# Sliding-window attention and a soft mixture of experts on one core: four-head steps, a single pass of dispatch scores, and a table of sequences

## The chip, the cores and the metric

One NeuronCore of a Trainium2 chip runs the whole program in one launch. The metric is the time of one execution on the device in microseconds. Lower is better. Inputs and outputs are fp32, and lie in the chip's memory (HBM) before and after.

## What is computed

Attention over 4 batches, 8 heads, 768 tokens, 64 values per head, with 4 sink tokens and a window of 128, and then a soft mixture of 8 experts with 4 slots each:

```python
scores = q @ k.T / 8, kept where the key is a sink (0..3) or 0 <= query - key < 128
x = softmax(scores) @ v                      # 3072 tokens x 512
logits = x @ phi                             # 3072 x 32 slots
d = softmax(logits, axis=0)                  # dispatch: over the tokens
c = softmax(logits, axis=1)                  # combine: over the slots
slot_in = d.T @ x                            # 32 x 512
slot_out = relu(slot_in @ w1[e]) @ w2[e]     # 8 experts, F = 1024
out = c @ slot_out                           # 3072 x 512
```

The weights w1 and w2 are 33.5 MB, the queries, keys and values 18.9 MB, the output 6.3 MB.

## The kernel before, in words

The attention is cut into 12 jobs of 256 queries (4 batches times 3, `jobs`). For each job the program adds steps to a planner, `Plan`, in `window_path`:

- `load`: two loads of 128 rows each for keys, for queries and for values, all 8 heads wide (256 KB each). For the first job keys and queries are loaded before the plan, by four heads.
- `prep`: 64x64 transposes of the keys on TensorE into two PSUM banks (32 of them), two copies of 512 columns out of them to `kt`; the same for the queries to `qt`. For later thirds of a batch, a copy of the last 128 key columns to the front, `kt0`. In the first job these are 128x128 transposes.
- `softmax`, four times per job (two halves of the tokens for each four heads, `quad`): scores on TensorE (`S`), mask and row maximum on DVE (`M`), four exponentials on ACT (`E`), then for a pair of them the inverse sums on DVE and the normalisation on POOL or ACT (`N`), and the sinks on POOL (`K0`).
- `weights_transposed` (`T`), `select` (affine selects on POOL that mask the transposed weights) and `sinks_transposed` (`K`).
- `values`: the product with V, one step of 52 fp32 matmuls for all eight heads. Two row groups of the array add into the same banks, so it is done in two passes with a drain of TensorE between them (`go`).
- `natural`: transposes of x back; `Moe.tokens`: the job's dispatch scores and products. `logits` writes the same 32 slots twice into PSUM, once for the plain logits (rows 0 to 63) and once for the exponential (rows 64 to 127); each sums four 128-value pieces of d, so 16 fp32 matmuls. DVE takes the maximum and then the minimum with the running one, ACT copies one half, exponentiates the other with the maximum as bias (`lt`), TensorE transposes `lt`, and `products` gathers d.T @ x, which DVE adds to `acc`.

`Plan.order` sets the order on every engine: it simulates the engines with the costs written at each step, and picks among the ready steps by due times from the table `CFG` (as `'val': [10.65, -12.08, -64.87]`). It keeps PSUM banks in reserve so that no step blocks. `issue` emits the steps in that order, so every engine has a fixed sequence in the program. Steps marked 900 and over are idle matmuls.

After the last job `finish` merges the slots' sums, nine `stack`/`turn` steps split the combine weights on POOL and transpose them on TensorE, and `tail` runs the experts: `first` (w1), `second` (w2) and `combine`, with 32 weight tiles of 1 MB that SP loads in a fixed order between the other loads. Tiles that take over the place of attention's buffers have to wait for the last readers of these (the last `values` for the transposed weights and V). Output leaves in 16 DMAs of 256 KB and 4 of 512 KB.

In the profile all steps of the plan carry line 136, the recorder's line; tiles tell them apart: `first,phi` are the logits, `wt,qt` the scores, `pts` the probabilities, `wt` the transposed weights, keys, V and expert weights, `pst,vsink` the sinks' part of the product with V, `ident,first` the transposes of keys, queries and x, `first,lb` the products.

Of the kernel before, what the change touches and what calls it, by code (L numbers as in the profile page):

```python
# [19 lines left out]
P = 128  # L20
# [47 lines left out]
def gate(nc, plan, c, phi, tmp, name):  # L68

    t = tmp.rearrange("p (k s) -> p k s", k=4)  # L70

    def sort(e):
        for k in range(4):
            nc.vector.tensor_copy(c.phi[:, k, :].rearrange("p (j r s) -> p j r s", j=4, r=2),
                                  t[:, k, :].rearrange("p (r j s) -> p j r s", r=2, j=4))

    plan.add(-1.0, "D", 0.4, lambda e: nc.sync.dma_start(t, phi.rearrange("(c p) s -> p c s", p=P)), w=[name])
    plan.add(7.0, "V", 0.34, sort, r=[name], w=["phi"])


def sink_values(nc, plan, pool, tmp, c, v, v4s):
# [28 lines left out]
    plan.add(1.5, "D", 2.0, load, w=["v4"])  # L110
    plan.add(1.0, "V", 0.9, selectors, w=["srow", "bm"])
    plan.add(1.0, "P", 0.45, lambda e: nc.tensor.matmul(
        h["tile"][:, 0:B * 64], lhsT=tmp[0:32, 512:640],
        rhs=v4.rearrange("p b d -> p (b d)"), start=True, stop=True), r=["srow", "v4"], w=["v4p"], new=h)
    plan.add(1.0, "A", 0.3, lambda e: nc.scalar.copy(hi, h["tile"][:, 0:B * 64]), r=["v4p"], w=["v4h"])
    plan.add(1.0, "V", 0.8, split, r=["v4p", "v4h", "bm"], w=["v4s"], last=h)
# [33 lines left out]
class Plan:  # L150

    LAT, DMA_LAT, SWITCH, STAY = 0.25, 1.8, 0.1, 2.0

    IDLE = 900.0  # L160
    BLOCK, FETCH = 256, 3.9

    def __init__(self, banks):

        self.banks, self.steps, self.modes, self.sizes, self.handles = banks, [], [], [], 0
# [9 lines left out]
    def add(self, key, eng, time, fn, r=(), w=(), new=None, last=None, mode=(128, 128), size=0):  # L175

        self.sizes.append(size)
        self.steps.append((key, eng, time if isinstance(time, tuple) else (time,) * len(eng), fn,
                           tuple(r), tuple(w), self.some(new), self.some(last)))
        self.modes.append(mode if isinstance(mode[0], tuple) else (mode, mode))  # L180

    def order(self):
        steps = self.steps
        writer, readers = {}, {}
        before, opener, later = [], {}, {}
        for i, (_, eng, _, _, r, w, new, last) in enumerate(steps):
            d = set()
            for x in r:
                d.add(writer.get(x, i))
                if x in opener:  # L190

                    d.update(readers.get(x, ())[-1:])
                readers.setdefault(x, []).append(i)
# [6 lines left out]
            for h in new:  # L200
                opener[h["name"]] = i

            for x in r + w:
                if x in opener and eng != "P":
                    o = opener[x]
                    later.setdefault(o, set()).update(y for y in d if steps[y][1] == "P" and y != o)
# [4 lines left out]
        ends = dict.fromkeys(closers, 0.0)  # L211
        nxt, left, ready = [[] for _ in steps], [len(d) for d in before], [0.0] * len(steps)
        for i, d in enumerate(before):
            for x in d:
                nxt[x].append(i)
        free = {"P": 5.3, "A": 5.5, "V": 5.5, "G": 6.8, "D": 3.1}
        todo = {e: [] for e in free}
        banks = dict.fromkeys(range(8), 0.0)
        for i, n in enumerate(left):
            if n == 0:  # L220
                for e in steps[i][1]:
                    todo[e].append(i)
        order, done, mode, place, since = [], set(), (128, 128), 0, 0.0
        while len(order) < len(steps):
            best = None
            for e, o in todo.items():
                at, t0 = [], 1e9
                for i in o:
                    t = max(free[e], ready[i])
                    new = steps[i][6]  # L230
                    if new:
                        free2 = sorted(banks.values())
                        if new[0]["kind"] == "s":
                            m, x = 2, min((max(banks[y], banks[y + 1]) for y in range(0, 8, 2)
                                           if y in banks and y + 1 in banks), default=None)
                        else:
                            m = len(new)
                            x = free2[m - 1] if len(free2) >= m else None
                        if x is None or len(free2) - m < 2 and not later.get(i, done) <= done:
                            continue  # L240
                        t = max(t, x)
                    at.append((t, i))
                    t0 = min(t0, t)
                if at and (best is None or t0 < best[0]):
                    if e == "P":
                        _, t, i = min((steps[i][0] + self.STAY * (self.modes[i][0] != mode), t, i)
                                      for t, i in at if t <= t0 + 0.1)
                    else:
                        _, t, i = min((steps[i][0], t, i) for t, i in at if t <= t0 + 0.02)
                    best = (t0, e, t, i)  # L250
            _, e, t0, i = best
            at = t0
            if e == "P":
                t0 += self.SWITCH * (self.modes[i][0] != mode)
                mode = self.modes[i][1]
            _, engs, times, _, _, _, new, last = steps[i]
            done.add(i)
            for x in engs:
                todo[x].remove(i)
            for h in new:  # L260
# [4 lines left out]
                else:  # L265
                    b = max((x for x in banks if banks[x] <= at + 1e-9),
                            key=lambda x: (x ^ 1 not in banks, banks[x], -x))
# [3 lines left out]
            end = t0 + times[engs.index(e)]  # L271
            place += self.sizes[i]
            if place >= self.BLOCK:
                place -= self.BLOCK
                t = end - (end - t0) * place / self.sizes[i]
# [9 lines left out]
            for x in nxt[i]:  # L285
                ready[x] = max(ready[x], end + (0.05 if steps[x][1] == e else self.DMA_LAT if e == "D" else self.LAT))
                left[x] -= 1
                if left[x] == 0:
                    for y in steps[x][1]:
                        todo[y].append(x)  # L290
# [3 lines left out]
    def issue(self):  # L294
        order = sorted(self.order())
        end = max(t for t, _, i, e in order if e == "P" and self.steps[i][0] < self.IDLE)
        for t, _, i, e in order:
            _, _, _, fn, _, _, new, _ = self.steps[i]
            if t > end and self.steps[i][0] >= self.IDLE:
                continue  # L300
# [16 lines left out]
class InOrder(Plan):  # L317

    at = 2
# [16 lines left out]
class Moe:  # L336
# [25 lines left out]
    def tokens(self, plan, keys, b, j, x, xn, blocks):  # L362
# [11 lines left out]
        both = len(blocks) == 2  # L374
# [964 lines left out]
```

## Time and profile before

| | |
|---|---|
| runs | 231.95, 234.34 and 232.90 us, median 232.9 |
| profiled execution | span 231.4 us, from its first to its last instruction; its own time is not listed beside the runs |
| TensorE busy | 196.0 us, 85% of the span |
| ACT, DVE, POOL busy | 151.9, 147.1 and 126.0 us |
| DMA engines, share of the span | 83.7% on the queue of the loads and stores |
| granted clock of TensorE | 0.969 in the mean |

How to read it: a "busy" time is the union of an engine's instructions. PE is the matmuls, PEld the weight loads, which overlap them; the ends of matmuls are modelled, so short gaps do not show under PE and do under PEld. A window row gives busy microseconds (and instructions) of each engine in a stretch, then the granted clock, the share of the DMA engines and GB/s.

### The profile page before, as it was taken

How to read it: one execution, taken by the hardware profiler on the slowest of the kernel's cores; microseconds unless marked ns; L12 is line 12 of the kernel's file. 1: busy time of each engine (PE TensorE's matmuls, PEld its weight loads, DVE VectorE, ACT ScalarE, POOL GpSimd, SP SyncE). 2: the span in 40 equal slices, each digit the busy share in tenths (PEclk: the TensorE clock that was granted, in tenths of full speed). 3: DMA queues.
4: the chain of work that ended last, by engine and by line, in shares of the span. 5: the costliest groups of instructions: out<-in, count | busy, mean ns of one | idle time of the engine just before them, and what ended most of it. 6: DMA issues, size and time to landing. Idle time of an engine off the chain costs nothing.

```text
span 231.4 us, 9764 instructions
## 1 busy us (share of the span) xinstructions
PE 196.0 (85%) x3912; PEld 144.0 (62%) x3912; DVE 147.1 (64%) x383; ACT 151.9 (66%) x605; POOL 126.0 (54%) x266
## 2 busy tenths in 40 slices
PE   7857998999898999899898889989699999999300
PEld 7836685867676777758577667667476235667200
DVE  5177787796868899797967788689526123017500
ACT  2297898889797987799986889989425113016400
POOL 2029698857769683957967395887973330000000
PEclk9997999999999999999999999999999999999955
DMA  5498969897989699896988889695549999986995
GB/s 114 95 218 200 291 159 302 253 266 203 225 249 241 202 289 322 233 211 211 213 338 197 268 183 298 178 428 224 203 157 423 370 426 390 347 259 224 303 350 227
DMA packets 90921, 59.53 MB, mean 257 GB/s; under 512 B 76532, under 2 KB 84724, under 8 KB 89332
## 3 DMA queue, kind: packets, MB, share of 16 engines
q1 hardware_dynamic: 90868, 58.83, 83.7%
q8 instruction: 33, 0.54, 0.9%
q14 instruction: 20, 0.16, 0.2%
HBM read 52.53 MB, written 6.29 MB: 254 GB/s over the span
## 4 chain that ended last, share of the span: by engine, by line
PE 51%; ACT 17%; DVE 12%; issue 7%; POOL 6%; DVEq 0%; ACTq 0%; POOLq 0%
PE ps L136 50%; ACT pts L136 8%; ACT wt L136 3%; DVE ps L136 3%; DVE small L136 2%; POOL pts L136 2%; ACT first L136 2%; DVE wt L136 2%; POOL wt L136 2%; PE ps L1291 2%; ACT lt L136 1%; DVE vsink L136 1%; DVE qt L136 1%; ACT qt L136 1%; DVE first L136 1%
## 5 line engine op out<-in xcount | busy, mean ns | idle before, releaser
L136 ACT ACTIVATE pts<-ps,small 128x132 f32<-128x132 f32 x192 | 68.1, 392 | 6.1 <-DVE small L136 3.4
L136 POOL TENSOR_SCALAR_AFFINE_SELECT wt<-wt 128x512 f32<-128x512 f32 x88 | 52.8, 634 | 3.0 <-ACT wt L136 1.2
L136 POOL TENSOR_TENSOR pts<-pts,small 128x528 f32<-128x528 f32 x36 | 38.2, 1076 | 29.3 <-DVE small L136 20.9
L136 PE MATMUL ps<-wt 64*64 64x192 f32 (+4 forms) x1278 | 52.5, 298 | 1.6 <-issue 0.3
L136 PEld LDWEIGHTS ps<-wt 64*64 64x64 f32 (+2 forms) x1278 | 38.9, 129 | 12.5 <-issue 4.8
L136 PE MATMUL ps<-wt,qt 64*64 64x196 f32 (+2 forms) x780 | 43.0, 325 | 4.0 <-ACT qt L136 1.4
L136 ACT ACTIVATION_READ_ACCUMULATOR pts<-ps,small 128x1 f32 x192 | 43.9, 229 | 0.0
L136 PEld LDWEIGHTS ps<-wt,qt 64*64 64x64 f32 x780 | 29.7, 135 | 11.3 <-ACT pts L136 2.4
L136 DVE TENSOR_REDUCE small<-ps 128x4 f32<-128x528 f32 x48 | 33.9, 707 | 1.6
L136 ACT COPY wt<-ps 128x512 f32<-128x512 f32 x39 | 23.1, 603 | 8.6 <-PE ps L136 8.5
L136 PE MATMUL ps<-ident,first 64*128 64x64 f32 (+1 forms) x560 | 25.1, 229 | 2.9 <-ACT pts L136 1.4
L136 DVE COPY wt<-ps 128x512 f32<-128x512 f32 x33 | 22.3, 682 | 4.8 <-ACT wt L136 2.1
L136 PEld LDWEIGHTS ps<-ident,first 64*128 64x128 f32 (+1 forms) x560 | 21.8, 141 | 5.2 <-issue 2.6
L136 DVE COPY first<-ps 128x512 f32<-128x512 f32 x24 | 16.4, 682 | 12.7 <-PE ps L136 12.4
L136 PE MATMUL ps<-ident,pts 64*128 64x64 f32 (+1 forms) x396 | 20.2, 233 | 3.7 <-DVE wt L136 2.1
L136 DVE COPY_PREDICATED ps<-later,ps 128x256 f32<-128x256 uint8 x48 | 20.3, 423 | 4.3 <-PE ps L136 3.4
L136 ACT COPY first<-ps 128x512 f32<-128x512 f32 x24 | 14.7, 610 | 12.2 <-PE ps L136 7.3
L136 PEld LDWEIGHTS ps<-ident,pts 64*128 64x128 f32 (+1 forms) x396 | 16.3, 142 | 9.7 <-POOL small L136 5.6
L136 ACT ACTIVATE pts<-pts,small 128x132 f32<-128x132 f32 x48 | 15.9, 437 | 0.6 <-DVE small L136 0.6
L136 PE MATMUL ps<-wt,si 128*32 128x512 f32 x120 | 14.1, 594 | 0.2 <-DVE si L136 0.2
L136 POOL TENSOR_TENSOR small<-pts,small 128x32 f32<-128x32 f32 x48 | 12.1, 252 | 3.9
L136 PE MATMUL ps<-first,phi 128*32 128x128 f32 x384 | 13.0, 276 | 0.1
(122 smaller groups left out, 240.1 us busy)
## 6 DMA issues: line engine op xcount, KB each, us to landing
wt<-in_moe_w_dram SPq DMA_DIRECT2D x26, 1024.0 KB, 6.9
wt<-in_v_dram SPq DMA_DIRECT2D x24, 256.0 KB, 4.5
first<-in_k_dram SPq DMA_DIRECT2D x22, 256.0 KB, 3.7
first<-in_q_dram SPq DMA_DIRECT2D x22, 256.0 KB, 4.7
wt<-in_moe_w_dram SPq DMA_DIRECT2D x8, 512.0 KB, 10.2
out_dram<-wt SPq DMA_DIRECT2D x16, 256.0 KB, 4.5
first<-in_moe_w_dram SPq DMA_DIRECT2D x2, 1024.0 KB
out_dram<-wt SPq DMA_DIRECT2D x4, 512.0 KB, 5.3
```

What stands on the lines that cost most here:

```text
L136: return self.tc.keep_in_program_order(f(*args, **kw))
L1291: nc.tensor.matmul(t[:, 0:P], lhsT=c.ident, rhs=c.ident, start=True, stop=True)
```

## The change

- Keys and queries are loaded by four heads (128 KB each, `load_keys`); one `prep` step transposes keys and queries of four heads together, with four copies of 256 columns instead of two of 512 for each. The first job takes the same path.
- `values` becomes two steps, one per four heads. The first needs neither the sinks nor the other four heads. Each has its own drain.
- `logits` runs once: rows 0 to 63 hold the sum over the first two pieces of d, rows 64 to 127 that over the other two. ACT copies one half to `lt`, DVE adds the halves, negates and takes the running minimum in one operation, reads it out and copies it to the other 64 partitions; ACT then exponentiates from `lt`. The combine softmax works on the negated logits.
- The greedy planner and its `CFG` give way to `ORDER`, a sequence of step numbers for each engine. The 24 idle matmuls before the experts are gone. Costs written at the steps matter for the bank numbers and the emission order only.

```diff
 def logits(e):
-    for a in range(4):
+    for a in range(2):
         for g in range(4):
-            nc.tensor.matmul(L["tile"][32 * g:32 * g + 32, 0:P], lhsT=c.phi[:, a, :],
-                             rhs=xt[:, a, x[g % 2 if both else blocks[0]]], start=(a == 0), stop=(a == 3),
-                             skip_group_check=True)
+            d = 2 * (g // 2) + a
+            nc.tensor.matmul(L["tile"][32 * g:32 * g + 32, 0:P], lhsT=c.phi[:, d, :],
+                             rhs=xt[:, d, x[g % 2]], start=(a == 0), stop=(a == 1), skip_group_check=True)
...
+def total(e):
+    nc.vector.tensor_tensor_reduce(lt[0:64], L["tile"][0:64, 0:P], lt[0:64], -1.0, old[0:64] if n else BIG,
+                                   ALU.add, ALU.min, new[0:64])
+    nc.vector.tensor_copy(new[64:128], new[0:64])
-plan.add(key, "V", 0.2, lambda e: nc.vector.tensor_reduce(
-    new, L["tile"][:, 0:P], op=ALU.max, axis=AX.X, negate=True), r=[L["name"]], w=[("m", n % 2)])
...
-plan.add(next(k), "A", 0.16, lambda e: nc.scalar.copy(lt[0:64], L["tile"][0:64, 0:P]), r=[L["name"]], w=["lt0"])
+plan.add(next(k), "A", 0.16, lambda e: nc.scalar.copy(lt[0:64], L["tile"][64:128, 0:P]), r=[L["name"]], w=["lt0"])
+plan.add(key, "V", 0.32, total, r=[L["name"], ("m", (n + 1) % 2)], w=["lt0", ("m", n % 2)], last=L)
...
+def load_keys(nc, t, src, b, j, quad):
+    for i in range(2):
+        s0 = 256 * j + P * i
+        nc.sync.dma_start(t[:, i, 256 * quad:256 * quad + 256].rearrange("p (h d) -> p h d", h=4),
+                          src[b, 4 * quad:4 * quad + 4, s0:s0 + P, :].rearrange("h p d -> p h d"))
...
+h = turned(keys[0], KIND["kt"], lambda rows, m: kqs[m // 4][rows, m % 2, P * (2 * quad + m // 2 % 2):P * (2 * quad + m // 2 % 2) + P],
+           [("kq", kind, quad) for kind in range(2)])
...
-def go(e):
-    for first in (True, False):
-        if not first:
+def go(e, quad):
+    for turn in range(2):
+        first = turn == quad
+        if turn:
             nc.tensor.drain()
-        for f in (sunk, part) if first else (part, sunk):
-            f(first)
+        for f in ((part, sunk) if turn else (sunk, part)) if quad else (part,):
+            f(*(quad, first) if f is part else (first,))
...
+ORDER = {"P": [
+         10, 11, 8, 12, 21, 9, 13, 35, 27, 38, 14, 16, 46, 7, 94, 49, 15, 2, 107, 100, 57, 110, 118, 60, 121,
...
```

What moves, first on TensorE in the third job, at its product with V (`ps<-wt` with widths 192, 64 and 128, each row four fp32 matmuls; `pst,vsink` is the sinks' part, `first_74` the keys and queries of later jobs, `ident,lt` the transposes of the dispatch scores). Before, from the middle of the product on:

```order
L136 MATMUL ps<-wt 64x192 x4
L136 MATMUL ps<-wt 64x64 x4
L136 MATMUL ps<-wt 64x128 x4
L136 MATMUL ps<-pst,vsink 128x256 x2
L136 MATMUL ps<-ident,lt 128x128
L136 MATMUL ps<-ident,first_74 128x64 x32
L136 MATMUL ps<-first_75,lb 32x257 x4
L136 MATMUL ps<-ident,pts 128x64 x16
```

and now, from the end of the first four heads' part to behind the second's:

```order
L136 MATMUL ps<-wt 64x128 x4
L136 MATMUL ps<-ident,first_74 128x64 x16
L136 MATMUL ps<-pst,vsink 128x256 x2
L136 MATMUL ps<-wt 64x192 x4
L136 MATMUL ps<-wt 64x64 x4
L136 MATMUL ps<-wt 64x128 x4
L136 MATMUL ps<-wt 64x192 x4
L136 MATMUL ps<-wt 64x64 x4
L136 MATMUL ps<-wt 64x128 x4
L136 MATMUL ps<-pst,vsink 128x256 x2
L136 MATMUL ps<-ident,first_74 128x64 x16
L136 MATMUL ps<-ident,lt 128x128
```

One block of 32 transposes of keys and queries behind the product has become two of 16, one between its two parts and one behind it.

Second, on TensorE from the merge of the slots' maxima (`sums,si`) to the experts (`wt,si`; `ident,pts` and `ident,qt` are the turns of the combine weights, `lt,acc` the slots' inputs, plain `ident` idle matmuls). Before:

```order
L136 MATMUL ps<-sums,si 128x1
L136 MATMUL ps<-ident,pts 128x128 x2
L136 MATMUL ps<-ident,lt 128x128
L136 MATMUL ps<-ident,qt 128x128 x2
L136 MATMUL ps<-first_75,lb 32x257 x4
L136 MATMUL ps<-ident,pts 128x128 x2
L136 MATMUL ps<-ident 128x128 x3
L136 MATMUL ps<-lt,acc 128x64 x2
L136 MATMUL ps<-rz,phi 128x1
L136 MATMUL ps<-wt,si 32x512 x48
```

and now:

```order
L136 MATMUL ps<-sums,si 128x1
L136 MATMUL ps<-ident,lt 128x128
L136 MATMUL ps<-first_75,lb 32x257 x4
L136 MATMUL ps<-ident,pts 128x128 x2
L136 MATMUL ps<-lt,acc 128x64 x2
L136 MATMUL ps<-ident,pts 128x128 x6
L136 MATMUL ps<-ident,qt 128x128 x4
L136 MATMUL ps<-ident,pts 128x128 x2
L136 MATMUL ps<-ident,qt 128x128 x2
L136 MATMUL ps<-rz,phi 128x1
L136 MATMUL ps<-wt,si 32x512 x48
```

Seven of the nine turns (14 transposes) now stand between the slots' inputs and the experts, where none stood; the idle matmuls are gone.

Third, on SP from the last loads of keys and queries (`first_74<-in_k_dram`, `in_q_dram`) to the outputs; a weight tile is one row `wt<-in_moe_w_dram` or `first...<-in_moe_w_dram`, and two halves of the last form, `128x4x256`. Before:

```order
L136 DMA first_74<-in_k_dram 128x8x64 x2
L136 DMA first_74<-in_q_dram 128x8x64 x2
L136 DMA wt<-in_v_dram 128x8x64 x2
L136 DMA wt<-in_moe_w_dram 128x2x1024
L136 DMA wt<-in_v_dram 128x8x64
L136 DMA first_74<-in_moe_w_dram 128x2x1024
L136 DMA wt<-in_moe_w_dram 128x2x1024
L136 DMA wt<-in_moe_w_dram 128x2048 x2
L136 DMA wt<-in_v_dram 128x8x64
L136 DMA wt<-in_moe_w_dram 128x2048 x4
L136 DMA first_75<-in_moe_w_dram 128x2048
L136 DMA wt<-in_moe_w_dram 128x2048 x5
```

and now:

```order
L136 DMA first_74<-in_q_dram 128x4x64 x2
L136 DMA wt<-in_v_dram 128x8x64
L136 DMA wt<-in_moe_w_dram 128x2x1024 x3
L136 DMA wt<-in_v_dram 128x8x64
L136 DMA wt<-in_moe_w_dram 128x2x1024
L136 DMA wt<-in_v_dram 128x8x64
L136 DMA wt<-in_moe_w_dram 128x2x1024
L136 DMA wt<-in_v_dram 128x8x64
L136 DMA wt<-in_moe_w_dram 128x2x1024 x2
L136 DMA wt<-in_moe_w_dram 128x2048 x4
L136 DMA first_74<-in_moe_w_dram 128x2048
L136 DMA wt<-in_moe_w_dram 128x2048
```

Both end with `first_75`, five tiles and eight halves. Before, 13 tiles are issued ahead of the last keys and queries and 18 ahead of the last V; now it is 9 and 14.

## Rows read from the trace of the kernel before

**Rows 1.** The page: span, and each engine's busy us, share and instructions.
```profile
span 231.4 us, 9764 instructions
PE 196.0 (85%) x3912; PEld 144.0 (62%) x3912; DVE 147.1 (64%) x383; ACT 151.9 (66%) x605; POOL 126.0 (54%) x266
```
**Rows 2.** Windows: us, busy (x) of PE, PEld, DVE, ACT, POOL; clock, DMA share, GB/s.
```profile
8.00:20.00 12.00, 7.74 (x140) 6.05 (x140) 7.89 (x25) 9.54 (x43) 4.15 (x8) 0.97 0.65 148
20.00:160.00 140.00, 128.64 (x2995) 99.41 (x2991) 112.45 (x270) 121.79 (x510) 103.73 (x210) 0.99 0.88 252
160.00:177.80 17.80, 15.35 (x293) 11.53 (x293) 9.80 (x30) 8.29 (x26) 13.04 (x32) 1.00 0.63 227
177.80:231.40 53.60, 37.84 (x454) 20.50 (x454) 13.83 (x33) 10.64 (x26) 3.83 (x7) 0.90 0.90 325
```
**Rows 3.** Waits from 20 to 160 us: PEld, in total, times, longest.
```profile
PEld ps L136 <- issue: 10.8, 36, 1.5
PEld ps L136 <- ACT pts L136: 6.1, 16, 1.0
PEld ps L136 <- POOL small L136: 5.6, 10, 1.0
PEld ps L136 <- POOL wt L136: 3.6, 7, 0.7
```
**Rows 4.** Groups by form: busy us, mean ns of one, idle before.
```profile
L136 PE MATMUL ps<-first,phi 128*32 128x128 f32 x384 | 13.0, 276 | 0.1
L136 ACT COPY wt<-ps 128x512 f32<-128x512 f32 x39 | 23.1, 603 | 8.6 <-PE ps L136 8.5
L136 DVE COPY wt<-ps 128x512 f32<-128x512 f32 x33 | 22.3, 682 | 4.8 <-ACT wt L136 2.1 <-PE ps L136 2.0 <-POOL small L136 0.6
L136 ACT CAST pts<-ps 128x256 fp32r<-128x256 f32 x3 | 1.1, 374 | 1.8 <-PE ps L136 1.8
L136 DVE CAST pts<-ps 128x256 fp32r<-128x256 f32 x3 | 1.2, 413 | 0.0
L136 ACT ACTIVATE pts<-pts,small 128x132 f32<-128x132 f32 x48 | 15.9, 437 | 0.6 <-DVE small L136 0.6
L136 POOL TENSOR_TENSOR pts<-pts,small 128x528 f32<-128x528 f32 x36 | 38.2, 1076 | 29.3 <-DVE small L136 20.9 <-ACT pts L136 6.7 <-ACT call L136 1.8
L136 DVE TENSOR_REDUCE sums<-ps 128x1 f32<-128x128 f32 x12 | 3.4, 285 | 3.0 <-PE ps L136 2.6 <-ACT pts L136 0.5
L136 DVE SCALAR_TENSOR_TENSOR acc<-acc,sums,ps 128x257 f32<-128x257 f32 x11 | 5.2, 472 | 1.0 <-PE ps L136 0.9
L136 ACT COPY lt<-ps 64x128 f32<-64x128 f32 x12 | 3.1, 258 | 1.6 <-DVE sums L136 1.6
```
**Rows 5.** Timeline of the weight loads: start us, us, behind a product's drain.
```profile
79.28 0.85 PEld L136 LDWEIGHTS ps<-wt 64*64 64x64 f32 x29 [0.35 <-issue]
```
**Rows 6.** Timeline of SP: start us, us, loads of keys, queries, phi.
```profile
1.51 0.42 SPq L1280 DMA_DIRECT2D first<-in_k_dram  x1
5.27 0.51 SPq L1280 DMA_DIRECT2D first<-in_q_dram  x1
11.21 0.99 SPq L136 DMA_DIRECT2D first<-in_k_dram  x2
```
**Rows 7.** Timeline of TensorE: first transposes, end of the last job, experts.
```profile
7.81 0.60 PE L136 MATMUL ps<-ident,first 128*128 128x128 f32 x4
175.96 0.44 PE L136 MATMUL ps<-ident,pts 128*128 128x128 f32 x2
208.78 1.93 PE L136 MATMUL ps<-wt 128*32 128x256 f32 x32
```
**Rows 8.** Windows at the experts: the columns of rows 2.
```profile
165.00:170.00 5.00, 3.78 (x104) 2.88 (x106) 1.01 (x3) 0.50 (x3) 4.47 (x11) 1.00 0.03 8
190.00:195.00 5.00, 5.00 (x55) 1.96 (x45) 1.72 (x5) 1.26 (x3) 0.00 (x0) 1.00 1.00 410
206.00:208.70 2.70, 2.70 (x36) 1.97 (x28) 1.20 (x3) 0.95 (x2) 0.00 (x0) 1.00 0.32 104
```

More of the change, by code (lines that the diff above doesn't have):

```diff
@@ L175, in add, with depends @@
     def add(self, key, eng, time, fn, r=(), w=(), new=None, last=None, mode=(128, 128), size=0):
[L177 to L186, printed above, removed]
+        self.steps.append((key, eng, time if isinstance(time, tuple) else (time,) * len(eng), fn, tuple(r), tuple(w),
+                           self.some(new), self.some(last), mode if isinstance(mode[0], tuple) else (mode, mode), size))
+    def depends(self):
+        writer, readers, before = {}, {}, []
+        for i, (_, _, _, _, r, w, new, _, _, _) in enumerate(self.steps):
             d = set()
+            opens = {h["name"] for h in new}
             for x in r:
                 d.add(writer.get(x, i))
-                if x in opener:
+                if x in self.opened:
                     d.update(readers.get(x, ())[-1:])
@@ L199, in order @@
             before.append(d)
[L200 to L206, printed above, removed]
+            self.opened |= opens
+        return before
+    def order(self):
+        steps, self.opened = self.steps, set()
+        before = self.depends()
+        nxt, left, ready = [[] for _ in steps], [len(d) for d in before], [0.0] * len(steps)
+        for i, d in enumerate(before):
+            for x in d:
+                nxt[x].append(i)
         closers = {}
@@ L210, in order @@
                 closers[h["name"]] = closers.get(h["name"], 0) + 1
[L211 to L223, printed above, removed]
+        ends, free, banks = dict.fromkeys(closers, 0.0), dict(self.START), dict.fromkeys(range(8), 0.0)
+        todo = {e: list(reversed(o)) for e, o in ORDER.items()}
+        on = {i: e for e, o in ORDER.items() for i in o}
+        order, mode, place, since = [], (128, 128), 0, 0.0
         while len(order) < len(steps):
@@ L226, in order @@
             for e, o in todo.items():
[L227 to L243, printed above, removed]
@@ L256, in order @@
[L256 to L259, printed above, removed]
+                if not o or left[o[-1]]:
+                    continue
+                i = o[-1]
+                t, new = max(free[e], ready[i]), steps[i][6]
+                if new:
+                    if new[0]["kind"] == "s":
+                        x = min((max(banks[y], banks[y + 1]) for y in range(0, 8, 2) if y in banks and y + 1 in banks), default=None)
+                    else:
+                        x = sorted(banks.values())[len(new) - 1] if len(banks) >= len(new) else None
+                    if x is None:
+                        continue
+                    t = max(t, x)
@@ L260, in order @@
+                if best is None or t < best[0]:
+                    best = (t, e)
+            at, e = best
+            i, t0 = todo[e].pop(), at
+            _, eng, times, _, _, _, new, last, modes, size = steps[i]
+            time = times[eng.index(e)]
+            if e == "P":
+                t0 += self.SWITCH * (modes[0] != mode)
+                mode = modes[1]
             for h in new:
@@ L294, in issue @@
     def issue(self):
[L295 to L300, printed above, removed]
+        for _, _, i, e in sorted(self.order()):
+            _, _, _, fn, _, _, new, _, _, _ = self.steps[i]
             for h in new:
@@ L814, in load @@
         b, j = jobs[n]
[L815 removed]
+        s0 = 256 * j
         if kind == 2:
[L817 to L827 removed]
@@ L829, in prep @@
[L829 to L840 removed]
+            x = (2 * n + i) % 4
@@ L881, in softmax @@
+                add(keys[1 + 2 * kind + x], "AV", (0.27, 0.33), out, r=[h[x]["name"]],
+                    w=[("q" if kind else "kt", quad, x)], last=h[x])
+        if j == 0:
+            add(keys[6], "G", 0.22, lambda e: nc.gpsimd.tensor_copy(
+                ktb[:, a, 1:3, 0:4], ktb[:, a, 1:2, 4:8].to_broadcast([P, 2, 2, 4])),
+                r=[("kt", quad, 0)], w=[("kts", quad)])
     def softmax(keys, n, tl):
@@ L1103, in window_path @@
     for i in range(NSLOT - 7):
-        add(O["w"][0] + O["w"][1] * i, "D", 3.0, lambda e: weight())
-    add(100.0, "D", 3.0, lambda e: weights.load(moe.first[0]), w=[("kq", x, i, y) for x in range(2) for i in range(2) for y in range(2)])
-    add(100.0, "D", 3.0, lambda e: weight(),
-        w=["kt0", ("kts", 0), ("kts", 1), "v4s"] + [("kt", i, y) for i in range(2) for y in range(2)])
-    add(100.0, "D", 0.0, lambda e: moe.place(
+        add((f"w.{i}", 0, 0.0), "D", 2.6, lambda e: weight())
```

328 lines of the change are left out of this document (119 added, 209 removed), and 53 rows, old and new, of the table ORDER.

## The prediction, before the changed kernel ran

> **What bounds the kernel now.** I read the page first, then windows by stage, the waits of the middle stage, the groups by form, and last the timelines of single steps.
>
> The page [rows 1] shows TensorE busy for 85% of the span and no other engine over 66%. The windows [rows 2] show where. From 20 to 160 us, eleven of the twelve jobs, TensorE is busy 128.6 of 140 us (92%), ACT 121.8 (87%), DVE 112.5, POOL 103.7, and the DMA engines 88%. From 8 to 20 us TensorE has 4.3 us idle, in the last job (160 to 177.8) 2.4. So before the experts start at 177.8 it stands still for 11.4 + 4.3 + 2.4 = 18.1 us in all, and whatever shortens its own work in the middle is worth nearly its full length. The reader should also look at the weight loads, since ends of matmuls are modelled: PEld is busy only 99.4 of the 140 us. What ends its idle time [rows 3] is spread: 10.8 us "issue", then waits of a few tenths for probabilities on ACT (6.1), sinks on POOL (5.6), selects on POOL (3.6). There is no one late engine. The experts and the output, 177.8 to 231.4, are TensorE until some 2 us past 208.78 [rows 7] and mostly DMA afterwards; the change edits nothing in there but the order of the tiles.
>
> **The change part by part.** The sum is made against the profiled span of 231.4. The runs have a median of 232.9, so 1.5 is added at the end; the lowest run, 231.95, would make that 0.6.
>
> *Logits.* 384 records in 12 groups of 32 become 192. They are 13.0 us busy [rows 4], 1.08 a job. Half is 6.5 us of TensorE. At the 92% at which the engine is busy I count 5.9 as path: -5.9.
>
> *Product with V in two.* The matmuls stay, but there are two drains per job instead of one. The one drain shows as a gap of 0.35 us in the weight loads [rows 5]; some of it may be covered by matmuls still running, so twelve more cost between 0 and 4.2 us. I take 3.0, nearer to the row: +3.0. So half of what the logits give is handed back. Each drain is paid by TensorE itself; nothing else can run in it.
>
> *First job and start-up.* 16 transpose records of 128 columns (the last four took 0.60 from 7.81 [rows 7]) become 32 short ones, about even. More important, keys and queries of the second job can be loaded as soon as four heads of the first are transposed, about 8.5 us, where SP issued them at 11.2 [rows 6] behind phi and five loads of values. In the 4.3 us of idle time from 8 to 20 I give this 2: -2.0 (bounds 0 and -4.3).
>
> *Copies.* 48 copies of 512 columns become 96 of 256. ACT takes 0.60 for 512 and 0.37 for 256, DVE 0.68 and 0.41 [rows 4]. The order gives ACT 46 instead of 24 (+2.6 us) and DVE 50 instead of 24 (+4.2). ACT also takes five more of the 512-column copies of x (+3.0, DVE -3.4), but 16 fewer normalisations of 15.9/48 = 0.33 each (-5.3); those go to POOL as four of 1.08 (+4.3), and the boundary copies `kt0` are now halves, at most 0.5 each by POOL's rate for 528 columns, which adds up to 4 us more there. ACT comes out even, DVE at +1, POOL at +4 to +8. What hides it is their idle time from 20 to 160, 18, 27 and 36 us [rows 2]. Without that cover DVE and POOL would cost what they add.
>
> *Running maximum.* No row shows the fused operation. It reads PSUM and SBUF at 128 columns; the nearest rows are the reduction of 128 columns, 0.285, and the three-operand operation of 257, 0.472 [rows 4]. I take 0.3, with a read-out and a 64-row copy of at most that each. Twelve jobs then have 6 to 10.8 us of it on DVE where the reductions had 3.4, at most 7.4 more, hidden as above. The chain is longer: ACT's copy (0.26 [rows 4]) ran beside the reduction and now goes first, so the exponential starts about 0.5 later. Queued behind the waiting operation on DVE are the masks of the next scores, for which ACT's exponentials wait; on TensorE scores stand between logits and transposes, which covers it in the middle. In the last job nothing does: +0.5.
>
> *Packing.* What is left is the order. The first four heads' product no longer waits for the last selects or the sinks, keys and queries of four heads are replaced while the other four are in use. That touches the waits on POOL's selects and sinks and part of those on ACT [rows 3], 9.2 to 15.3 us of weight-load idle, of which perhaps half is true idle of TensorE. Bounds: zero, and the whole 11.4 us idle of the middle. I take 4.5, nearer to the rows on POOL: -4.5.
>
> *End.* Seven turns now stand between the slots' inputs and the experts. A turn is two transposes, 0.44 us alone and 0.30 when packed (four took 0.60) [rows 7], so seven are 2.1 us. They left the gaps between the steps of this chain, where TensorE now waits, so they count up to their length; against that stands the copy of the slots' inputs to SBUF, which they cover, and what TensorE waits there now: +0.5 (bounds -0.5 and +2.1). The shorter logits of the last job are counted above.
>
> *Weights.* 9 tiles instead of 13 are issued ahead of the last keys and queries, 14 instead of 18 ahead of the last V. The DMA engines idled at 3% from 165 to 170 [rows 8], so two of the four fit there (1.05 MB at 410 GB/s [rows 8] is 2.6 us), if their buffers are free then, and more before it. The last tiles land shortly after 206 and are used at 208.78 [rows 7, 8]: 2 us of slack. I take +0.5, between 0 and the 8 of the rival below.
>
> Sum: -5.9 + 3.0 - 2.0 + 0.5 - 4.5 + 0.5 + 0.5 = -7.9. The span would be 223.5, the median of the runs 225.0.
>
> *A rule against it.* The eight loads of 128 KB at the start were issued 0.54 apart, from 1.51 to 5.27 [rows 6], and the transposes of the last of them ran at 7.81 [rows 7]: all were in within some 2 us of the last issue, so they overlapped. The change makes 88 loads of this size out of 44 of 256 KB. The Trainium skill (DMA: Bandwidth & Descriptors, "Anatomy of one DMA" and "Rules for kernel authors") asks for 1 MB and more per DMA and gives about 2 us fixed for each on its software-issued path; paid one after the other, 44 more would be 88 us by estimate. By the rows the fixed part overlaps, and the sum has nothing for it.
>
> **The rivals.**
>
> *TensorE stands between the two parts (slower).* Its sequence is fixed: when the first part is done and 16 transposes behind it, the second waits for the selects of the other four heads, whatever else is ready. POOL runs these last and has 4 to 8 us more to do. For it: the waits on POOL's selects exist already, 3.6 us in 7 times, 0.5 each [rows 3]. Against: POOL has 36 us of slack. Price: 0.6 us in each of 11 jobs, +6.6, and the packing gain of 4.5 does not come: 231.4 - 7.9 + 4.5 + 6.6 = 234.6, runs 236. It decides from an average wait of 0.3 at the second part: with the packing gone that leaves 3.3 + 4.5 against 7.9, no gain.
>
> *The weights come late.* Four tiles more behind the last V are 10.2 us of DMA. If their buffers are only freed by the last product with V, they do not fit into the idle time, and the expert products stall by 10.2 - 2 = 8 us; TensorE's gain is then hidden by the transfers: 231.4 - 8.4 + 8 = 231.0, runs 232.5. For it: from 177.8 on the DMA engines are 90% busy [rows 2]. Against: most of these tiles have buffers of their own. One tile late costs at most 0.6.
>
> *The order packs better.* If two thirds of the 18.1 us of idle time go, that is 12 instead of 6.5: 218, runs 219.5. For it: the steps are finer everywhere. Against: twelve jobs with waits of 0.3 to 0.6 on four engines need a nearly perfect agreement of planned and real times.
>
> *The order does nothing.* Logits and drains alone, -2.9, and +1.5 of the small terms, without a gain at the start: 230, runs 231.5. Here the change does its work on TensorE but the idle time moves elsewhere.
>
> **How the numbers follow.** Forecast, 222 to 229 in the runs: 0.55. Better packing: 0.14. No gain from the order: 0.09. Late weights: 0.08. Standing between the parts: 0.14. About 1% is what a measurement of this kernel tells from no change, 2.3 us. Faster by over 1% (below 230.6): the forecast and the better packing with a fifth of the next two cases, 0.73. Within 1%: most of these two, 0.12. Slower: 0.15, nearly all from the rival at TensorE. The range from 218.5 to 234 leaves out the far end of the better packing and most of the slower case.
>
> **What would show it.** Right: TensorE's busy time before the experts falls by some 3 to 5 us, logits show 192 records and 6.5 us; weight loads show two gaps of about 0.35 per product; the experts start near 170; idle time of TensorE before that falls from 18 to about 12. The fused maximum takes 0.3 to 0.5 on DVE. Wrong: a row of waits of TensorE on POOL's selects of some 6 us or more (first rival); stalls of TensorE on "issue" or DMA while `wt,si` or the `128x256` matmuls of the experts run, with the DMA engines full (second); experts at 175 or later with no single wait (last). The forecast fails as well if the jobs' pace is set by ACT, busy over 92% from 20 to 150.

## The result, and the profile after

| | before | after |
|---|---|---|
| median of 20 runs each, us | 234.09 | 231.58 |
| lowest to highest | 231.75 to 238.25 | 228.64 to 236.28 |
| ratio, 95% interval | | 0.9868 (0.9835 to 0.9902) |
| profiled execution: its time, span | span 231.4 | 230.66, span 228.9 |

The change makes the kernel 1.3% faster, where I had forecast 3.4% (225.0). Shares and ratios below are of runs taken beside runs of the kernel before; executions that were disturbed are left out of the ratios.

The page of the changed kernel, as [rows 1]:

```profile
span 228.9 us, 9482 instructions
PE 198.2 (87%) x3730; PEld 138.1 (60%) x3730; DVE 149.0 (65%) x413; ACT 153.4 (67%) x620; POOL 133.1 (58%) x281
```

Its windows in the stretches of [rows 2] (busy us of PE, PEld, DVE, ACT, POOL; clock; DMA share; GB/s):

```profile
8.00:20.00 12.00, 10.70 (x194) 7.58 (x194) 10.23 (x31) 9.68 (x45) 4.73 (x11) 1.00 0.66 149
20.00:160.00 140.00, 131.82 (x2948) 97.52 (x2949) 116.52 (x305) 127.11 (x535) 117.61 (x238) 1.00 0.86 237
160.00:177.80 17.80, 12.71 (x118) 7.10 (x122) 7.39 (x26) 4.65 (x15) 5.68 (x16) 0.72 1.01 415
177.80:228.90 51.10, 36.48 (x445) 19.75 (x434) 12.10 (x26) 10.29 (x25) 3.84 (x7) 0.90 0.89 314
```

TensorE is busier up to 160 us, and from 160 to 177.8 it does little, at a granted clock of 0.72 in the mean where it had 1.00. So I cut both traces at events instead: the end of the last product with V, the experts' first matmul, the experts' last `128x256` group. Before:

```profile
8.00:170.60 162.60, 145.06 (x3332) 111.86 (x3331) 125.69 (x307) 135.35 (x564) 116.70 (x236) 0.99 0.83 236
170.60:177.85 7.25, 6.68 (x89) 5.13 (x90) 4.51 (x16) 4.26 (x13) 4.22 (x12) 1.00 0.98 375
177.85:208.78 30.93, 30.93 (x386) 15.06 (x387) 6.75 (x22) 5.01 (x16) 3.83 (x7) 1.00 0.97 355
208.78:231.40 22.62, 6.91 (x69) 5.44 (x68) 7.03 (x12) 5.62 (x12) 0.00 (x0) 0.76 0.82 283
```

and after:

```profile
8.00:161.15 153.15, 143.66 (x3161) 105.94 (x3161) 126.75 (x335) 136.78 (x578) 122.86 (x249) 1.00 0.85 232
161.15:175.03 13.88, 8.79 (x78) 5.48 (x76) 6.33 (x23) 4.65 (x15) 5.15 (x14) 0.74 1.01 416
175.03:207.37 32.34, 32.34 (x387) 15.08 (x386) 6.11 (x19) 4.66 (x15) 3.84 (x7) 0.96 0.91 333
207.37:228.90 21.53, 6.91 (x69) 5.45 (x68) 7.04 (x12) 5.64 (x12) 0.00 (x0) 0.77 0.85 296
```

The whole result is in these rows. Attention, up to the end of the last product with V, is 9.45 us shorter; the way from there to the experts is 6.63 longer (13.88 against 7.25); the experts are 1.41 longer, the output 1.09 shorter. The sum is -2.5, the difference of the spans. The gain came, and two thirds of it were given back within 14 us.

Where it was given back shows on TensorE's timeline (`lt,acc` are the slots' inputs, `ident,pts` and `ident,qt` the turns of the combine weights, `wt,si` the experts):

```profile
160.77 0.38 PE L136 MATMUL ps<-pst,vsink 64*128 64x256 f32 x2
166.03 0.44 PE L136 MATMUL ps<-ident,pts 128*128 128x128 f32 x2
166.75 0.66 PE L136 MATMUL ps<-lt,acc 128*128 128x64 f32 x4 [0.29 <-DVE acc L136]
167.48 0.54 PE L136 MATMUL ps<-ident,pts 128*128 128x128 f32 x2
169.93 1.12 PE L136 MATMUL ps<-ident,pts 128*128 128x128 f32 x4 [1.91 <-POOL pts L136]
172.43 0.69 PE L136 MATMUL ps<-ident,qt 128*128 128x128 f32 x2 [0.95 <-POOL qt L136]
174.22 0.66 PE L136 MATMUL ps<-ident,qt 128*128 128x128 f32 x2 [0.33 <-ACT pts L136]
175.03 11.91 PE L136 MATMUL ps<-wt,si 128*32 128x512 f32 x96
```

and on POOL's, which splits the combine weights that TensorE then turns:

```profile
160.14 0.46 POOL L136 TENSOR_TENSOR pts<-call,pts 128x128 fp32r<-128x128 f32 x1
166.60 0.29 POOL L136 CAST pts<-call 128x128 fp32r<-128x128 f32 x1 [6.00 <-PE ps L136]
171.54 0.29 POOL L136 CAST qt<-call 128x128 fp32r<-128x128 f32 x1 [1.67 <-PE ps L136]
```

The slots' inputs are done at 167.41 and in SBUF at 167.74, so the experts could have begun less than a microsecond after them, as they do in the first experiment below. They stand behind the last turn in TensorE's sequence. The nine splits share three places in SBUF; a split may only overwrite a place after the turn that reads it. POOL had made two by 160.6 and then stood 6.00 us, because the second turn comes behind the last job's products in TensorE's fixed sequence (166.03). Seven splits were left, and POOL and TensorE took turns waiting for each other.

Windows of this stretch after, for the clock:

```profile
164.00:166.00 2.00, 0.95 (x10) 0.32 (x10) 1.54 (x7) 1.45 (x5) 0.00 (x0) 1.00 1.03 426
166.00:168.00 2.00, 1.64 (x12) 0.92 (x8) 1.47 (x5) 0.00 (x0) 1.24 (x4) 0.92 1.00 414
168.00:170.00 2.00, 0.09 (x2) 0.07 (x2) 1.01 (x3) 0.36 (x1) 1.72 (x5) 0.50 1.02 414
176.00:178.00 2.00, 2.00 (x16) 0.47 (x12) 0.09 (x2) 0.00 (x0) 0.00 (x0) 0.52 0.85 360
```

The granted clock is 0.50 (1.2 of 2.4 GHz) from 168 to 176. It fell shortly before 168, after TensorE had worked 0.95 of 2.00 us from 164 to 166 and 1.64 from 166 to 168; behind the fall stands the emptiest row, 0.09 us. A turn then takes 0.63 to 0.69 instead of 0.44 [rows 7], and the experts' first 96 matmuls 11.91 instead of 10.51.

Groups and waits that answer to [rows 3] to [rows 5]. PEld's waits from 20 to 160 us, the groups by form, and the weight loads behind the two drains of one job:

```profile
PEld ps L136 <- issue: 17.1, 60, 0.8
PEld ps L136 <- ACT pts L136: 4.7, 18, 0.8
PEld ps L136 <- POOL wt L136: 3.1, 7, 0.8
PEld ps L136 <- POOL small L136: 1.6, 5, 0.4
```

```profile
L136 PE MATMUL ps<-first,phi 128*32 128x128 f32 x192 | 7.7, 277 | 0.5 <-DVE first L136 0.3 <-DVE wt L136 0.2
L136 DVE CUSTOM_DVE_ANT_0 lt<-ps,lt,sums 64x128 f32<-64x128 f32 x11 | 3.7, 337 | 2.5 <-ACT lt L136 1.3 <-ACT sums L136 1.2
L136 DVE DVE_READ_ACCUMULATOR2_ANT sums<- 64x1 f32 x12 | 0.9, 75 | 0.0
L136 DVE COPY sums<-sums 64x1 f32<-64x1 f32 x12 | 1.8, 147 | 0.4
```

```profile
86.75 0.65 PEld L136 LDWEIGHTS ps<-wt 64*64 64x64 f32 x24 [0.34 <-issue]
89.38 0.65 PEld L136 LDWEIGHTS ps<-wt 64*64 64x64 f32 x24 [0.35 <-issue]
```

The waits for probabilities, sinks and selects fell, those on "issue" rose by 6.3 us with 24 more of them. The two gaps of 0.34 and 0.35 within one product are its two drains; the rows do not say what else the 24 are. The fused maximum is 0.34, with read-out and copy 0.56.

One more difference lies at the start. The granted clock of the kernel before fell there, behind waits of TensorE of 1.43 us (ahead of 16.48) and 0.97 (ahead of 18.16):

```profile
18.00:20.00 2.00, 1.42 (x28) 1.31 (x30) 1.76 (x9) 2.00 (x9) 1.92 (x4) 0.82 0.86 198
20.00:22.00 2.00, 1.88 (x33) 1.50 (x33) 1.29 (x3) 1.36 (x4) 1.76 (x7) 0.50 1.00 223
22.00:24.00 2.00, 2.00 (x40) 1.42 (x36) 1.23 (x3) 0.35 (x2) 2.00 (x5) 0.82 1.16 263
```

The changed kernel has 1.00 in all three.

### The profile page after: what moved, and what is told of

The parts are those of the page before. It is cut to its first block, busy times and chain, and to the rows that moved or that the text cites. A ratio compares the mean times of both kernels' runs of the same rounds, so it can differ in the third digit from the quotient of the medians.

```text
span 228.9 us, 9482 instructions
## 1 busy us (share of the span) xinstructions
PE 198.2 (87%) x3730; PEld 138.1 (60%) x3730; DVE 149.0 (65%) x413; ACT 153.4 (67%) x620; POOL 133.1 (58%) x281
## 5 line engine op out<-in xcount | busy, mean ns | idle before, releaser
L136 PE MATMUL ps<-wt 64*64 64x192 f32 (+5 forms) x1262 | 59.3, 300 | 4.7 <-DMA wt<-in_v_dram 1.0
L136 PEld LDWEIGHTS ps<-wt 64*64 64x64 f32 (+3 forms) x1262 | 40.3, 129 | 17.9 <-issue 8.3
L136 POOL TENSOR_TENSOR pts<-pts,small 128x528 f32<-128x528 f32 x40 | 42.3, 1071 | 14.3 <-DVE small L136 12.8
L136 ACT COPY wt<-ps 128x512 f32<-128x512 f32 (+1 forms) x49 | 24.1, 509 | 10.2 <-PE ps L136 8.7
L136 DVE COPY wt<-ps 128x256 f32<-128x256 f32 (+1 forms) x47 | 24.9, 536 | 6.5 <-ACT wt L136 3.7
L136 PE MATMUL ps<-ident,first 64*128 64x64 f32 x576 | 26.1, 228 | 1.1 <-DMA first<-in_k_dram 1.0
L136 PEld LDWEIGHTS ps<-ident,first 64*128 64x128 f32 x576 | 21.3, 140 | 7.5 <-issue 2.6
L136 DVE COPY first<-ps 128x512 f32<-128x512 f32 x19 | 12.9, 685 | 9.3 <-PE ps L136 8.4
L136 PE MATMUL ps<-wt,si 128*32 128x512 f32 x128 | 15.6, 642 | 0.0
L136 POOL COPY wt<-wt 128x256 f32<-128x256 f32 (+1 forms) x21 | 6.8, 327 | 11.3 <-ACT wt L136 8.5
L136 ACT ACTIVATE pts<-pts,small 128x132 f32<-128x132 f32 x32 | 10.5, 421 | 0.7 <-DVE small L136 0.7
```

Of the source, the lines that this page charges most:

```text
L136: return self.tc.keep_in_program_order(f(*args, **kw))
```

## Experiments

The theory: attention gained what was forecast, and the turns took it, by POOL's waits and the low clock they cause. Rivals: the weights are the limit at the end; the last job's own chain is; the attention gain is something else than logits and order. The last is tested for the logits and the drains alone: no run separates the four-head steps and loads, the product in two and the new table from one another.

**The turns spread over the last job.** Edit of the changed kernel's table, ends of two sequences (copies follow the same order):

```diff
 "P": [
...
-898, 899, 836, 956, 905, 838, 902, 917, 910, 912, 959, 921, 965, 962, 971, 974, 977, 968, 980, 924
+898, 899, 836, 956, 959, 905, 974, 838, 902, 965, 917, 962, 977, 910, 971, 912, 968, 980, 921, 924
 "G": [
...
-955, 958, 964, 973, 970, 961, 976, 967, 979
+955, 958, 973, 964, 961, 976, 970, 967, 979
```

> The changed kernel with the nine turns of the combine weights spread between the last job's steps (five of them ahead of the slots' inputs, and the other copies and splits in the same order), nothing else. Theory (the turns behind the slots' inputs ate the gain): POOL makes its splits from 159 to about 167 with no wait over 1 us for TensorE, the experts' first matmul starts at 168 to 170 instead of 175.0, the granted clock stays at 1.0 until there, span 222 to 224, time 5 to 7 us below the changed kernel's 231.6. Rival 1 (the weights are the limit: the DMA engines are full from 158 to 176): the experts start early but stand still for weights, time 229 to 231. Rival 2 (the last job's chain is the limit, not the turns): the experts start at 173 or later, time within 1 us of 231.6.

Measured: 227.39 us, ratio 0.9754 (0.9698 to 0.981), span 225.7. TensorE:

```profile
166.87 0.66 PE L136 MATMUL ps<-lt,acc 128*128 128x64 f32 x4
168.35 10.51 PE L136 MATMUL ps<-wt,si 128*32 128x512 f32 x96
192.31 5.08 PE L136 MATMUL ps<-wt 128*32 128x256 f32 x57 [1.97 <-DMA wt<-in_moe_w_dram]
```

POOL's longest wait of the row (0.55 us; another of 0.30):

```profile
161.31 0.29 POOL L136 CAST pts<-call 128x128 fp32r<-128x128 f32 x1 [0.55 <-PE ps L136]
```

The experts start 6.7 us earlier, with a full clock and their 96 matmuls at 10.51. Attention ends 0.6 earlier (160.54); the way from there to the experts is 7.81 instead of 13.88, near the 7.25 of the kernel before. So the turns were the cause, and the first part of the theory holds. But the span falls by only 3.2, less than I expected. The 96 matmuls end 8.1 us earlier (178.86 against 186.94), the last `128x256` group starts 3.1 earlier (204.30 against 207.37): 5.0 us are lost in between. There TensorE stands for weights, 2.2 us in all around 190, and the granted clock falls behind that wait to 0.60 and 0.54 (192 to 196). The first rival was not what limited the changed kernel, but it is the next limit.

**One turn alone.** Of the same edit only step 959 (the turn for which POOL waited 6.00) moved behind 956, its copy with it.

> The changed kernel with one step moved: the turn for whose room POOL waits 6.0 us is put right behind the turn ahead of it, with its copy. If that one wait is the cause, POOL's wait goes and the experts start at 170 or earlier, time 226 to 227. If it is the whole row of turns behind the slots' inputs (each split waits for the turn before it in its room), POOL does two more splits early and then waits for the next turn until about 167.5: the experts start at 173.5 to 175, time within 1.5 us of 231.6.

Measured: 233.06 us, ratio 0.9931 (0.9886 to 0.9975). POOL:

```profile
166.69 0.29 POOL L136 CAST pts<-call 128x128 fp32r<-128x128 f32 x1 [1.39 <-PE ps L136]
173.56 0.29 POOL L136 CAST pts<-call 128x128 fp32r<-128x128 f32 x1 [5.26 <-PE ps L136]
```

The wait splits into 1.39 and 5.26; the experts start 14.6 us after the last product (13.9 without the edit). One wait removed shows the next in the same row. (In this profiled execution attention ends 4.7 us later, at 165.85, with 2.6 us of TensorE's waits for loads of queries between 66 and 84 us, so only its end is compared.)

**Idle matmuls instead.** Eleven matmuls of the identity put into the waits of the changed kernel's last stretch, no turn moved.

> The changed kernel with 11 idle matmuls (128 columns, as the kernel before had) in TensorE's waits of the last stretch: 3 ahead of the last products, 5 behind the third turn, 2 and 1 between later turns. Theory (the granted clock fell to 0.5 there because TensorE had nothing to do, and that made turns 0.63 instead of 0.44 and the experts' first 96 matmuls 11.9 instead of 10.5 us): the clock stays at 1.0 up to the experts, these start 0.5 to 1.5 us earlier and their 96 matmuls take 10.5; time 2 to 3 us below 231.6. If the clock falls anyway, or the idle matmuls delay the turns by what they save: within 1 us.

Measured: 228.75 us, ratio 0.9812 (0.9749 to 0.9875), span 225.9.

```profile
173.63 10.51 PE L136 MATMUL ps<-wt,si 128*32 128x512 f32 x96 [0.47 <-DVE qt L136]
```

```profile
168.00:170.00 2.00, 1.11 (x11) 0.92 (x10) 1.31 (x6) 0.36 (x1) 1.11 (x3) 1.00 1.03 414
```

The clock stays at 1.00 through the stretch, the 96 matmuls take 10.51, and the way from the last product to the experts is 13.1 instead of 13.9. By the trace that is 2.2 us (1.4 + 0.8) of the 3.0 by which the span is shorter; most of the rest is attention. The ratio's interval overlaps that of the changed kernel. The low clock was part of the loss. The removal of the idle matmuls alone does not bring it, the waits do: of the 24 steps the kernel before ran three here (0.83 us at 176.24), and with the turns spread none runs and the clock is 1.00 from 160 to 190.

**Weights earlier.** Three tiles taken from behind the last V and planned at 75, 84 and 96 us (with the turns spread they are issued at 76.3, 87.9 and 97.5), first with the turns spread, then with the changed kernel's own turns:

```diff
 "D": [
...
-937, 542, 484, 406, 543, 541, 544, 617, 485, 618, 558, 615, 616, 696,
+937, 542, 944, 484, 406, 543, 541, 544, 939, 617, 485, 618, 558, 615, 616, 935, 696,
```

> The turns spread as in the first experiment (227.4 us, span 225.7), and three weight tiles of 1 MB that already had buffers of their own taken from behind the last loads of V to the idle stretches of the DMA engines at 75, 84 and 96 us. Theory (with the turns gone from the path, the weights are next: TensorE stood 2.2 us for DMA and the engines were full from 155 to 201): the waits on weights go, the last expert products end 2 to 2.5 us earlier, span about 223.3, time 225. Rival (the early tiles collide with the loads of keys and queries of jobs 8 and 9, and these with TensorE): attention ends 1 to 2 us later, time 227 to 229.

> The changed kernel with the same three tiles moved, and the turns left as they are. If the changed kernel's end was limited by turns and not by weights: no gain, 231.6 within 1 us. If late weights were the cause of the lost gain (my rival of late weights): 3 us or more faster.

Measured with the turns spread: 225.40 us, ratio 0.9663 (0.9604 to 0.9722), span 222.0; no wait of TensorE on weights is left. Attention ended 1.4 us later than without the tiles (161.91), as the rival had it, but the time was the theory's.

```profile
190.00:200.00 10.00, 10.00 (x180) 6.16 (x171) 0.65 (x2) 0.77 (x2) 0.00 (x0) 1.00 1.01 323
```

Without: four runs from 229.96 to 237.47, too scattered for a ratio; the profiled span is 228.0 against 228.9, the experts start 13.9 us after the last product as before, and take 12.15 for the 96. So the same three tiles are worth 2.0 us by the medians once the turns are off the path (3.7 by the two profiled spans, but 223.79, the time of the one with tiles, is the lowest of its six runs; the intervals of the two ratios overlap); with the turns still on it they are worth no more than a microsecond by the profiled spans. A variant with two tiles at 84 us instead:

> As the turns with early weights (225.4 us, span 222.0), but the tile that stood at 75 us moved to 84, so that two tiles lie in the longest idle stretch of the DMA engines (84 to 90 us). There the fifth product with V ended 2 us later than without it (79.1 against 77.1) and attention 1.4 later in all. If that early tile held up the loads of queries: attention ends at about 160.5 instead of 161.9, span 220.5 to 221.5, time 224. If two tiles in a row hold up the next loads of V and queries instead: the same or 1 us slower.

Measured: 226.21 us, 0.9668 (0.962 to 0.9716): no difference. Attention ended at 163.3, not earlier; the second alternative.

**The scores twice, and a third drain.** Two edits of the changed kernel that take one term of the sum back each: `for a in (0, 1, 0, 1)` in `logits`, and a `drain` ahead of the second part of the product.

> The changed kernel with each job's dispatch scores issued twice into the same bank (16 fp32 matmuls as before the change, the second eight overwrite the first). If TensorE sets the pace in the middle (my term of -5.9 for the logits): +6 us, time 237.5, between 236.5 and 238.5. Rival (another engine sets the pace, ACT is busy 91% of the middle): 0 to +2.

> The changed kernel with one more drain of TensorE per job, between the two parts of the product with V. My term: 0.25 each, +3.0 us in all (bounds 0 and +4.2). If the drains are covered by matmuls that still run, or by waits at the second part that come anyway, 0 to +1.

Measured: 236.21 us, ratio 1.0112 (1.0031 to 1.0193), which is 0.0244 or 5.7 us over the changed kernel; by the profiled span +4.0 (232.9). The third drain: 234.13 us, 0.9972 (0.9918 to 1.0026), 0.0104 or 2.4 us over it. In the trace of the doubled scores attention ends 2.9 us later (164.04). Together the intervals leave about 2 us on either side of the 5.7 and 1.5 of the 2.4 (an estimate from the ratios above). So the scores are worth 4 to 6 us in the new order and a drain per job some 2.4, near the 5.9 and 3.0 of the sum.

**The scores once, in the old order.** The kernel before with its planner and only `tokens` and the sign of the combine softmax exchanged:

> The kernel before with its planner, its step times and its eight-head steps, and of the change only the dispatch scores issued once with the fused running maximum. If the logits' term (-5.9) holds by itself: 234.1 - 5.5 = 228.5, between 227.5 and 230. If the old order turns the saved TensorE time into other waits: 231 to 234.

Measured: 246.83 us, ratio 1.0544 (1.0485 to 1.0602). A planner may have made a new order of it, so the next kernel has the old sequences written out, and only the operations in them changed:

> The kernel before with every engine's sequence frozen as its planner made it (the same steps in the same places on every engine, banks by the same simulation), and of the change only the dispatch scores issued once, with the fused running maximum in the place of the two reductions. TensorE is 6.5 us less busy. If my logits term holds by itself, without a new order: the end of the eleventh product with V moves from 160.3 to about 155.5, time 234.1 - 5.5 = 228.5. If the fixed order keeps TensorE waiting at the same places for the other engines, and only a new order turns shorter steps into time: 232 to 234, with more waits of TensorE on ACT and POOL. The previous run without a frozen order (246.8) was the planner's new order then, not the operations.

Measured: 248.92 us, ratio 1.0607 (1.0545 to 1.0668). So a loss of this size needs no new order: the operations in the old sequence are enough. ACT and DVE of this kernel around 82 us:

```profile
81.33 0.24 ACT L136 ACTIVATION_READ_ACCUMULATOR pts<-ps,small 128x1 f32 x1
81.60 0.26 ACT L136 COPY lt<-ps 64x128 f32<-64x128 f32 x1
```

```profile
81.90 0.34 DVE L136 CUSTOM_DVE_ANT_0 lt<-ps,lt,sums 64x128 f32<-64x128 f32 x1 [1.99 <-ACT lt L136]
83.00 0.42 DVE L136 COPY_PREDICATED ps<-later,ps 128x256 f32<-128x256 uint8 x1
```

DVE's fused maximum now needs ACT's copy, and that stands behind two rows of exponentials. DVE waits 13.9 us so, up to 2.0 at a time, and the masks of the next scores wait behind it. The first run lost its time elsewhere. Its DVE waits 0.7 us for the copy, and the ends of its eleventh and twelfth products lie 20.8 us apart (165.03 and 185.79) where the kernel before has 10.3: its planner put the turns ahead of the last product, and the granted clock was 0.50 there from 172 to 184. That is 10.5 of its 14 us, and it is the planner's order, as I had read it. The group of the fused maximum in the first run, the second, and the third, which follows:

```profile
L136 DVE CUSTOM_DVE_ANT_0 lt<-ps,lt,sums 64x128 f32<-64x128 f32 x11 | 3.7, 336 | 0.7 <-ACT lt L136 0.7
L136 DVE CUSTOM_DVE_ANT_0 lt<-ps,lt,sums 64x128 f32<-64x128 f32 x11 | 3.8, 343 | 13.9 <-ACT lt L136 13.9
L136 DVE CUSTOM_DVE_ANT_0 lt<-ps,lt,sums 64x128 f32<-64x128 f32 x11 | 3.7, 340 | 3.3 <-ACT lt L136 3.3
```

To test the wait, the copy alone was moved ahead on ACT:

> As the frozen order of before with dispatch scores issued once (248.9 us), but ACT's copy of half of the scores taken out from behind the exponentials, to where ACT is free when the scores are done (it passes one or two steps of ACT in most jobs); every other sequence as before. There DVE's fused maximum stood 13.9 us in all for that copy, up to 2.0 in a job, with the masks of the next scores behind it. If that wait is what costs 14 us: it falls to under 4 us in all, and time to 228.5 to 231 (the logits' term of 5.9 less what the longer chain still costs). If the longer chain itself (copy, fused maximum, read-out, copy, then the exponential) stops the old order: 240 or more.

Measured: 237.72 us, ratio 1.0172 (1.0088 to 1.0256), span 233.0. DVE's waits for the copy fell to 3.3 us and 11 us came back, so the wait is the cause of most of it. But neither expectation is met: the eleventh product ends at 159.9 against 160.3 in the kernel before, with the scores' 5.3 us of TensorE gone. From 8 us to there TensorE is busy 135.6 us where it was 136.7, and idle 16.3 where it was 15.6: the group of the `wt,qt` scores, whose ends are modelled, now takes 44.2 instead of 41.0, and the idle time grew. What holds it there was not separated further; the longer chain, the copy's place and the old sequence are still together in this kernel. The rest of its loss is in the last job (the last product took 4.73 us at half clock, against 3.21).

## Why the prediction was wrong

The direction was right, the size less than half. By the steps of the sum:

- *Logits, second drain, start-up, packing*: -5.9 + 3.0 - 2.0 - 4.5 = -9.4 was forecast for attention, -9.45 was measured. That is partly luck. Logits and drains should have taken 2.9 us of TensorE's work: it fell by 1.4. Start-up and packing should have taken 6.5 us of its idle time: up to the last product that went from 17.5 to 9.5, 8.0 less.
- In the work, the scores' busy time fell by 5.3 (13.0 to 7.7), not 6.5, since a group of 16 records takes 0.64. The drains cost some 3.1 (the four groups of the product sum to 73.2 us after and 70.1 before), as forecast. One part had no term, the granted clock from 18 to 24 us (0.82, 0.50 and 0.82 before, 1.00 now). By the same forms in the kernel before at either level (1.45 against 0.71 for 16 transposes of probabilities, 2.07 against 1.56 for 32 scores, 1.07 against 0.71 for 16 transposes of keys and queries) that is an estimate of 1.6 us of TensorE's work.
- In the idle time, the start-up can't be read apart: from 8 to 20 us the idle time fell from 4.3 to 1.3, yet the first product ends at 29.1 against 29.3, and the second at 40.4 against 42.3.
- The terms don't add as I wrote them. Half the logits was counted as gain at the 92% at which TensorE is busy (6.0 by that, where I wrote 5.9). In the old sequence, with the longer chain, it gives nothing that shows, in the new one 4 to 5.7 us. As far as these runs go, *logits* and *packing* are one term, and the sequences decide what of it becomes time.
- *Running maximum*, +0.5 with a 0.5 us longer chain: the operations are 6.7 us on DVE, within what I gave. That the exponential's chain is covered in the middle holds in the new sequence, where DVE waits 1.3 us for ACT's copy; with the copy's old place in the old sequence the program was 14 us longer. I had named what is queued behind the waiting operation, but not what stands ahead of the one it waits for.
- *End*, +0.5 with bounds -0.5 and +2.1: the step that failed. Measured +6.63, of which the spread turns give back 6.1 (13.88 to 7.81). I priced the seven turns as TensorE's time (0.30 each) and took the copy of the slots' inputs as their cover. A turn is the second half of a pair; the first half, the split on POOL, is 0.75 us, and splits wait for the turns of their place. Seven splits behind 166.6 are 5.3 us of POOL before any wait. The order rows showed the turns behind the slots' inputs; POOL's sequence and the shared places were not read beside them.
- The granted clock had no term. With TensorE waiting between the turns it fell: +1.4 in the experts, and 0.8 in the turns (within *End*).
- *Weights late*, +0.5: nothing in the changed kernel. As a rival (8 us) it did not show, since the experts started late; with the turns spread TensorE waits 2.2 us for them. *TensorE stands between the two parts*: its waits on POOL's selects are 3.1 us from 20 to 160 [rows 3: 3.6]; that rival fell. *The order does nothing* gave 231.5, the number that came, by another mechanism: the order gained 8 us and lost 6.6.
- Of the signs for being right, TensorE's busy time before the experts did not fall by 3 to 5 us but rose by 0.7 (151.7 to 152.5), and the experts began at 175.0, not near 170. One reading was short as well: the experts' part of TensorE does not end 2 us past 208.78, where 6.9 us of its work follow.

On the clock, the Trainium skill (TensorE: Matmul & The Clock Gate, "What's actually happening") says that the low level is the default and that activity releases it. This trace agrees: 0.50 in the row from 168 to 170 us, in which TensorE had 0.09 us of work, and 1.00 in the same place with eleven idle matmuls in the stretch, 1.11 us of work in the row.

## What to carry to other kernels

When a table fixes every engine's sequence, price a moved step with its partner on the other engine and with the buffer both share: ask what must be freed before the partner can start, and follow that for the whole row; removing one wait of the row gave nothing here. Work taken off the busiest engine gave time here in the new sequences and none in the old, where a longer chain came with it, so make them again; and a new operand from another engine must come early in that engine's sequence. Look for the next limit as soon as one is gone: the turns and the weights together gave 225.4 us, 3.4% below the kernel before, the turns alone 2.5%.

## What was not expected of the hardware

- Idle matmuls on the critical stretch paid: eleven of them made the trace's last stretch and experts 2.2 us shorter, since the experts began at 1.00 instead of 0.50.
- DVE's wait of at most 2.0 us per job on a 0.26 us copy came with a program 14 us longer in the old sequence: the waits sum to 13.9, and moving the copy alone gave 11 back.
- 96 loads of 128 KB instead of 44 of 256 KB and 8 of 128 KB did no visible harm in the changed kernel's profile: TensorE's waits for keys are 1.0 us in all from 8 to 178, for queries none is listed. In the profile of the single moved turn it waited 2.6 us for queries.
